# Attention plus SoLU block on one core: VectorE's block turns write contiguous runs, and the readers of the result take strides

## The chip, the cores and the metric

The kernel runs on one core of a Trainium2 chip. The metric is the device time of one execution in microseconds (us). A core has TensorE (PE in the profile, its weight loads PEld), VectorE (DVE), ScalarE (ACT), GpSimd (POOL) and the queue that issues all transfers here (SP).

## The reference

Rotary attention of 4 x 8 heads over 576 positions of 64 elements, and then a two-layer block over the 2304 tokens that result:

```python
def rotate(x):
    x1, x2 = (x[..., :half], x[..., half:])
    return np.concatenate([x1 * cos - x2 * sin, x1 * sin + x2 * cos], axis=-1)
scores = scale * np.matmul(rotate(q), rotate(k).transpose(0, 1, 3, 2))
attn = softmax(scores)                      # max subtracted, 1e-9 in the sum
x = (attn @ v)  -> 2304 tokens x 512
h = x @ w_in                                # 512 -> 1024
solu = h * softmax(h)
ln = (solu - mu) / np.sqrt(var + 1e-06) * g_ln
out = ln @ w_out                            # 1024 -> 512
```

All inputs and outputs are float32.

## The kernel before, in words

**Attention.** Heads are taken in 16 pairs (P = 0 to 15), one head in the upper and one in the lower 64 partitions. For each pair there are four tiles of 128 queries per head and one packed tile with the last 64 queries of both heads. A tile's scores go to PSUM (tiles pd, lines 408, 430, 433), VectorE takes the negated row maximum (mx, line 388), and ScalarE writes the exponentials to SBUF (tiles e, line 390, keys along the free axis). The second product needs them with keys on the partitions, so each 128 x 512 block of e is turned into ET (four key groups m of 128 keys each) and the last 64 keys into EL. `av` (lines 509 to 527) then multiplies v by ET and EL into a PSUM tile pg, and VectorE scales the result with the reciprocal row sums Rb into xT (line 525), which holds the tokens of a batch along the free axis. `av` runs twice per pair: r = 0 for 256 queries and r = 1 for 320 (two tiles and the packed one).

**Two ways to turn a tile.** For pairs 0 to 3, TensorE transposes four 128 x 128 blocks into pg (`tr`, line 448) and a copy brings them to ET (line 318 where ScalarE copies, line 320 where VectorE does). For pairs 4 to 15 the turn goes over DRAM (line 467 writes e to escr in 32-row groups, line 468 reads it back regrouped), and VectorE finishes it with one STREAM_TRANSPOSE of 32 x 32 blocks (line 469). In those the source is read in steps of four words (`p (j b m)`, m inner), and the destination is written in steps of four words as well (`p m (a j)`, j inner), so that the queries come out in their natural order. The last 64 keys (EL, `turn_last`) go over TensorE and a copy in all pairs.

**The block behind it.** For each of 18 tiles of 128 tokens, `front` splits x into two parts xh and xl, multiplies by w_in (line 590), and computes the SoLU into u. u goes to DRAM (uscr) and comes back regrouped into wraw; `back` turns it with two STREAM_TRANSPOSEs into tiles tb (line 642: read contiguously, written in steps of four words), copies the first part (lnh, lines 318 or 320) and subtracts it for the second (lnl, line 652, on GpSimd or VectorE), multiplies by w_out (line 660), and scales into the output (line 665).

**What sets the order.** A planner fixed one list for all engines (`ORDER`), which engine takes an operation that two may do (`FLIP`), and which buffer each tile gets (`BUFS`). These tables are written out in the kernel, each engine works its part in that order, and the costs in the calls of `add` (1040 and 1050 ns for the two transposes) only served the planner.

Of the kernel before, what the change touches and what calls it, by code (L numbers as in the profile page):

```python
# [12 lines left out]
ALU = mybir.AluOpType  # L13
# [158 lines left out]
class Plan:  # L172
# [22 lines left out]
    def buf(self, use):  # L195
        return self.pools[self.uses[use][0]][self.uses[use][2]]

    def add(self, eng, cost, prio, fn, r=(), w=(), use=(), xfer=0.0, alt=None, two=False, mode=0):
        i = len(self.ops)
        if alt is not None:  # L200
            self.alts[i] = (eng, cost) + alt
        deps = set()
        for k in r:
            if k in self.lastw:
                deps.add(self.lastw[k])
        for k in w:
            if k in self.lastw:
                deps.add(self.lastw[k])
            deps.update(self.readers.get(k, ()))
        deps.discard(i)  # L210
        for k in w:
            self.lastw[k] = i
            self.readers[k] = []
        for k in r:
            if k not in w:
                self.readers.setdefault(k, []).append(i)
        self.tags.append(self.tag)
        self.two.append(two)
        self.modes[i] = mode
        uses = (use,) if isinstance(use, int) else tuple(use)  # L220
        for u in uses:
            self.uses[u][1] += 1
        self.ops.append((eng, cost, prio, fn, deps, uses, xfer))
        return i


def dve(n):
    return 69 + n / 0.96
# [6 lines left out]
def act(n, ptrs=0, psum=True):  # L235
    return (51 if psum else 93) + n / 1.2 + 93 * ptrs
# [7 lines left out]
def kernel(  # L244
# [13 lines left out]
    nc = tc.nc  # L258
# [16 lines left out]
    def st(shape, dt, name):  # L275
        return sb.tile(shape, dt, name=name)
# [12 lines left out]
    ET = [st([128, 2, 4, n], F32, f"ET{i}") for i, (_, n) in enumerate(RNG)]  # L289
    EL = [st([128, n], F32, f"EL{i}") for i, (_, n) in enumerate(RNG)]  # L290
    xT = st([128, KC, RING], F32, "xT")
    Rb = st([128, S], F32, "Rb")
# [21 lines left out]
    add, use, buf = pl.add, pl.use, pl.buf  # L314

    def copy(e, o, i):
        if e is nc.scalar:
            nc.scalar.copy(o, i)  # L318
        else:
            e.tensor_copy(o, i)  # L320
# [7 lines left out]
    def tau(P, un):  # L328
        return TP[P] + PT[P] * un / 9
# [46 lines left out]
    def attention(P):  # L376
        par = P % 2
        b, c = divmod(P, PB)
        xoff = (b % 2) * S
# [59 lines left out]
        def chunk(e, m):  # L439
            return e.rearrange("p (x m) -> p m x", m=4)[:, m, :]  # L440
# [13 lines left out]
        def turn_tile(i, h):  # L454
            jt = 5 * P + i
            ej = et[jt % NE]
            r, q0 = divmod(i, 2)
            q0 *= 128
            base = 0 if h == 0 else S + 64
            pl.tag = f"T{P}.{i}.{h}"  # L460
            t = tau(P, 2 * i + h)
            if (i, h) in OFFS[P]:


                e, ke = ej[:, base:base + 512], ("e", jt % NE, h)
                sc, ks = escr[P, i, h], ("es", P, i, h)
                dma(t, sc.rearrange("i p c -> p i c"), e.rearrange("p (i c) -> p i c", i=4), 0, [ke], [ks], xf=728.0)
                dma(t, e, sc.rearrange("i (a j) c -> (i a) (j c)", j=4), 0, [ks], [ke], xf=728.0)
                add("dve", 1040, t, lambda: nc.vector.transpose(  # L469
                    ET[r][:, h, :, q0:q0 + 128].rearrange("p m (a j) -> p j m a", j=4),  # L470
                    e.rearrange("p (j b m) -> p j m b", j=4, m=4)), [ke], [("E", r, h, i % 2, 0)])
                return

            def blocks(bt):
                return [(bt[:, 128 * m:128 * m + 128], chunk(ej[:, base:base + 512], m)) for m in range(4)]

            tr(tau(P, 2 * i + h), [("e", jt % NE, h)], blocks, 512,
               [(ET[r][:, h, :, q0:q0 + 128], lambda bt: bt.rearrange("p (m q) -> p m q", m=4))], ("E", r, h, i % 2))

        def turn_last(r):  # L480

            pl.tag = f"T{P}.{r}.l"
            js = [(5 * P + 2 * r + y) % NE for y in range(2)]

            def blocks(bt):
                return [(bt[:, 128 * y:128 * y + 128], et[js[y]][:, S - 64:S + 64]) for y in range(2)]

            tr(tau(P, 4 * r + 3), [("el", j, h) for j in js for h in range(2)], blocks, 256,
               [(EL[r][:, 0:256], lambda bt: bt[:, 0:256])], ("EL", r, 0))

        def turn_packed():
            jt = 5 * P + 4
# [16 lines left out]
        def av(r, t):  # L509
            q0, nq = RNG[r]  # L510
            pl.tag = f"A{P}.{r}"
            ek = {h: [("E", r, h, y, 0) for y in range(2)] + ([("E", 1, "P", 0)] if r else []) for h in range(2)}
            lk = [("EL", r, 0, 0)] + ([("EL", 1, "P", 0), ("EL", 1, "P", 1)] if r else [])
            uy = use("G")
            yk = ("Y", uy)
            for m in range(5):
                def AV(m=m):
                    for h, rows in ((0, A), (1, B)):
                        e = ET[r][:, h, m, :] if m < 4 else EL[r]
                        nc.tensor.matmul(buf(uy)[rows, 0:nq], vv[:, m, h, :], e, start=(m == 0), stop=(m == 4))  # L520

                keys = ek[0] + ek[1] if m < 4 else lk
                add("pe", 2 * (nq * 2 / 2.4 + 3), t, AV, keys + [("v", par)], [yk], use=uy, mode=3)

            add("dve", dve(nq), t, lambda: nc.vector.tensor_tensor(  # L525
                xT[:, c, xoff + q0:xoff + q0 + nq], buf(uy)[:, 0:nq], Rb[:, q0:q0 + nq], op=ALU.mult),
                [yk] + [("R", r, j) for j in range((2, 3)[r])], [("x", b % 2, c, r)], use=uy)

        def norm(r, t):
# [33 lines left out]
    kl = [[("lh", z)] for z in range(2)], [[("ll", z)] for z in range(2)]  # L563
# [59 lines left out]
    def back(i, t, dur, tail):  # L623

        r0 = 128 * i
        tl = t + dur * 0.7
        col, mk = msc(i)
        pl.tag = f"l{i}"  # L630
        v = wraw.rearrange("p (j c) -> p j c", j=4)
        add("sp", 500, tl, lambda: nc.sync.dma_start(wraw, uscr[i].rearrange("i (a j) c -> (i a) (j c)", j=4)),
            [("us", i)], [("wr",)], xfer=2100.0)
        for z in range(2):
            pl.tag = f"t{i}.{z}"
            ub = use("B")
            bk = ("tz", ub)

            def turned(ub=ub):
                return buf(ub).rearrange("p (m t) -> p m t", m=4)  # L640

            add("dve", 1050, tl, lambda z=z, turned=turned: nc.vector.transpose(  # L642
                turned().rearrange("p m (a j) -> p j m a", j=4),
                v[:, :, 128 * z:128 * z + 128].rearrange("p j (m b) -> p j m b", b=32)),
                [("wr",), ("tbfree",)], [bk], use=ub)
            hd, ld = lh[:, 4 * z:4 * z + 4, :], ll[:, 4 * z:4 * z + 4, :]
            add("act", act(512, psum=False), tl, lambda e, hd=hd, turned=turned: copy(e, hd, turned()), [bk], kl[0][z], use=ub,
                alt=("dve", dve2(512)), two=True)
            c = [("pool", pool(512)), ("dve", dve(512))]
            if tail and z:  # L650
                c.reverse()
            add(*c[0], tl, lambda e, hd=hd, ld=ld, turned=turned: e.tensor_tensor(ld, turned(), hd, op=ALU.subtract),  # L652
                [bk] + kl[0][z], kl[1][z], use=ub, alt=c[1], two=True)
        pl.tag = f"o{i}"
        uo = use("G")
        ok = ("op", i)
        for f in range(FC):
            def mm2(f=f):
                for j, (a, w) in enumerate(((lh, woh), (lh, wol), (ll, woh))):
                    nc.tensor.matmul(buf(uo), a[:, f, :], w[:, f, :], start=(f == 0 and j == 0), stop=(f == FC - 1 and j == 2))  # L660
            add("pe", 3 * 228, t + dur + dur * 0.5 * f / FC, mm2, kl[0][f // 4] + kl[1][f // 4] + [("wo", f)], [ok], use=uo)
        to = t + 1.5 * dur
        add("act", act(512, 1, psum=False), to, lambda: nc.scalar.activation(osb, wm, AF.Copy, scale=col(13)), [("wm",)] + mk(13),
            [("o",)])
        add("dve", dve(512), to, lambda: nc.vector.scalar_tensor_tensor(  # L665
            osb, buf(uo), col(14), osb, op0=ALU.mult, op1=ALU.add), [ok, ("o",)] + mk(14), [("o",)], use=uo)
        dma(to, out[r0:r0 + 128, :], osb, 128 * DM * 4, [("o",)], [("out", i)])
# [129 lines left out]
    with tc.manual_schedule():  # L797
        for i in ORDER:
            if i in pl.alts:
                a = pl.alts[i]  # L800
# [67 lines left out]
```

## Time and profile before

| | us |
|---|---|
| median of 3 runs | 467.17 |
| lowest, highest | 464.99, 470.39 |
| span of the profiled execution, from its first to its last instruction | 464.3 |
| VectorE busy in it | 406.7 |
| TensorE busy in it | 436.2 |
| ScalarE, GpSimd busy in it | 264.1, 200.9 |

The profile is of one execution. Its span is 2.9 us below the median of the runs, which contains what lies around the span. Busy time is the union of an engine's instructions; matmuls are pipelined and their ends are modelled, so TensorE counts as busy also where it is not at its peak.

### The profile page before, as it was taken

How to read it: one execution, taken by the hardware profiler on the slowest of the kernel's cores; microseconds unless marked ns; L12 is line 12 of the kernel's file. 1: busy time of each engine (PE TensorE's matmuls, PEld its weight loads, DVE VectorE, ACT ScalarE, POOL GpSimd, SP SyncE). 2: the span in 40 equal slices, each digit the busy share in tenths (PEclk: the TensorE clock that was granted, in tenths of full speed). 3: DMA queues.
4: the chain of work that ended last, by engine and by line, in shares of the span. 5: the costliest groups of instructions: out<-in, count | busy, mean ns of one | idle time of the engine just before them, and what ended most of it. 6: DMA issues, size and time to landing. Idle time of an engine off the chain costs nothing.

```text
span 464.3 us, 7958 instructions
## 1 busy us (share of the span) xinstructions
PE 436.2 (94%) x2688; PEld 310.5 (67%) x2688; DVE 406.7 (88%) x663; ACT 264.1 (57%) x597; POOL 200.9 (43%) x164
## 2 busy tenths in 40 slices
PE   1799999999999979999999999999999999999996
PEld 1456666677667755766667677666767676778885
DVE  3889999999989999899999999999999889796672
ACT  1568898888766557455646545464655544433421
POOL 1203342435778355437458465656365320102331
PEclk9989999999999999999999999999999999999999
DMA  7547465799879999999889899999799787643541
GB/s 240 184 145 241 146 221 179 235 265 315 261 229 298 287 282 276 291 324 301 282 239 305 260 292 309 294 321 286 241 272 327 242 244 234 201 139 114 158 160 46
DMA packets 96410, 112.42 MB, mean 242 GB/s; under 512 B 7649, under 2 KB 71153, under 8 KB 96369
## 3 DMA queue, kind: packets, MB, share of 16 engines
q1 hardware_dynamic: 96368, 111.91, 76.9%
q8 instruction: 21, 0.34, 0.3%
q14 instruction: 21, 0.16, 0.1%
HBM read 72.49 MB, written 39.40 MB: 241 GB/s over the span
## 4 chain that ended last, share of the span: by engine, by line
PE 25%; DMA 13%; DVE 11%; ACT 2%; issue 2%; SPq 1%; DVEq 0%; ACTq 0%
PE pg L660 9%; PE pd L590 9%; DMA escr<-e 5%; DMA e<-escr 4%; PE pg L520 3%; DVE ET L469 3%; PE pd L408 2%; DVE mx L388 2%; DMA wraw<-uscr 2%; DVE ms L597 1%; PE pg L448 1%; DMA Rb<-rscr 1%; DMA uscr<-u 1%; DVE tb L642 1%; ACT e L390 1%
## 5 line engine op out<-in xcount | busy, mean ns | idle before, releaser
L390 ACT ACTIVATE e<-pd,mx 128x576 f32<-128x576 f32 x144 | 106.2, 739 | 73.6 <-DVE mx L388 52.1
L469 DVE STREAM_TRANSPOSE ET<-e 128x512 f32<-128x512 f32 x96 | 105.6, 1132 | 8.9 <-DMA e<-escr 8.4
L388 DVE TENSOR_REDUCE mx<-pd 128x1 f32<-128x576 f32 x144 | 103.5, 743 | 8.1 <-PE pd L408 7.0
L520 PE MATMUL pg<-ET,vst 128*64 128x256 f32 (+1 forms) x512 | 71.5, 418 | 0.9 <-DVE o L665 0.4
L652 POOL TENSOR_TENSOR lnl<-tb,lnh 128x512 fp32r<-128x512 f32 x30 | 38.7, 1290 | 61.4 <-ACT lnh L318 33.7
L590 PE MATMUL pd<-wih,xh 128*128 128x512 f32 x144 | 60.1, 417 | 0.5 <-ACT e L390 0.5
L660 PE MATMUL pg<-woh,lnh 128*128 128x512 f32 x144 | 58.8, 408 | 1.1 <-DVE xT L525 0.4
L590 PE MATMUL pd<-wih,xl 128*128 128x512 f32 x144 | 56.5, 392 | 0.0
L660 PE MATMUL pg<-woh,lnl 128*128 128x512 f32 x144 | 56.3, 391 | 0.0
L590 PE MATMUL pd<-wil,xh 128*128 128x512 f32 x144 | 56.2, 391 | 0.0
L660 PE MATMUL pg<-wol,lnh 128*128 128x512 f32 x144 | 56.2, 390 | 0.0
L448 PE MATMUL pg<-idn,e 128*128 128x128 f32 (+1 forms) x272 | 50.3, 300 | 5.6 <-ACT e L390 2.7
L520 PEld LDWEIGHTS pg<-ET,vst 128*64 128x64 f32 x512 | 34.7, 138 | 26.4 <-issue 4.6
L448 PEld LDWEIGHTS pg<-idn,e 128*128 128x128 f32 (+1 forms) x272 | 36.7, 187 | 23.4 <-ACT e L390 5.6
L642 DVE STREAM_TRANSPOSE tb<-wraw 128x512 f32<-128x512 f32 x36 | 39.0, 1099 | 1.8 <-DMA wraw<-uscr 1.6
L408 PE MATMUL pd<-kh,qh 64*128 64x288 f32 x192 | 38.0, 344 | 1.7 <-ACT e L390 0.7
L408 PE MATMUL pd<-rotk,rotq 64*128 64x288 f32 x128 | 27.0, 502 | 10.7 <-DVE rotk L349 9.7
L349 POOL TENSOR_TENSOR rawk<-rawk,tabs 128x576 f32<-128x576 f32 (+1 forms) x21 | 29.2, 1397 | 12.5 <-DMA rawk<-in_k_t_dram 12.5
L660 PEld LDWEIGHTS pg<-woh,lnh 128*128 128x128 f32 x144 | 27.1, 188 | 9.5 <-issue 2.1
L590 PEld LDWEIGHTS pd<-wih,xh 128*128 128x128 f32 x144 | 27.1, 188 | 9.3 <-issue 2.1
L349 POOL TENSOR_TENSOR rawq<-rawq,tabs 128x576 f32<-128x576 f32 x20 | 28.8, 1448 | 10.5 <-DMA rawq<-in_q_t_dram 10.5
L599 ACT ACTIVATE u<-pd,ms 128x1024 f32<-128x1024 f32 x18 | 20.1, 1116 | 22.1 <-DVE ms L597 10.6
(101 smaller groups left out, 841.8 us busy)
## 6 DMA issues: line engine op xcount, KB each, us to landing
escr<-e SPq DMA_DIRECT2D x96, 256.0 KB
e<-escr SPq DMA_DIRECT2D x96, 256.0 KB
uscr<-u SPq DMA_DIRECT2D x18, 512.0 KB
wraw<-uscr SPq DMA_DIRECT2D x18, 512.0 KB
rawq<-in_q_t_dram SPq DMA_DIRECT2D x15, 576.0 KB
rawk<-in_k_t_dram SPq DMA_DIRECT2D x15, 576.0 KB
vst<-in_v_t_dram SPq DMA_DIRECT2D x16, 320.0 KB
out_dram<-o SPq DMA_DIRECT2D x18, 256.0 KB
```

Of the source, the lines that this page charges most:

```text
L349: add(*c[0], prio, lambda e: e.tensor_tensor(o, a, b, op=op), r, w, alt=c[1], two=True)
L388: add("dve", 672, t, lambda: nc.vector.tensor_reduce(mx[:, mcol:mcol + 1], buf(us)[:, :, 0:288], axis=AX.XY, op=ALU.max, negate=True), [sk ...
L390: add("act", 720, t, lambda: nc.scalar.activation(e.rearrange("p (z n) -> p z n", z=2), buf(us)[:, :, 0:288], AF.Exp, bias=mx[:, mcol:mcol ...
L408: nc.tensor.matmul(buf(us)[:, z, 0:288], a[rows, c0:c0 + 128], w[rows, 288 * z:288 * z + 288], start=(j == 0), stop=(j == len(terms) - 1))
L448: nc.tensor.transpose(dst, src, idn)
L469: add("dve", 1040, t, lambda: nc.vector.transpose(ET[r][:, h, :, q0:q0 + 128].rearrange("p m (a j) -> p j m a", j=4), e.rearrange("p (j b ...
L520: nc.tensor.matmul(buf(uy)[rows, 0:nq], vv[:, m, h, :], e, start=(m == 0), stop=(m == 4))
L590: nc.tensor.matmul(buf(uh)[:, z, :], a[:, c, :], w[:, c, HF * z:HF * z + HF], start=(c == 0 and j == 0), stop=(c == KC - 1 and j == 2))
L599: add("act", act(DFF, 2), tm, lambda: nc.scalar.activation(u, buf(uh), AF.Exp, bias=col(2), scale=1.0, accum_out=col(3)), hf + mk(2), ku + ...
L642: add("dve", 1050, tl, lambda z=z, turned=turned: nc.vector.transpose(turned().rearrange("p m (a j) -> p j m a", j=4), v[:, :, 128 * z:128 ...
L652: add(*c[0], tl, lambda e, hd=hd, ld=ld, turned=turned: e.tensor_tensor(ld, turned(), hd, op=ALU.subtract), [bk] + kl[0][z], kl[1][z], use ...
L660: nc.tensor.matmul(buf(uo), a[:, f, :], w[:, f, :], start=(f == 0 and j == 0), stop=(f == FC - 1 and j == 2))
```

## The change

The destination of each STREAM_TRANSPOSE is laid out as (j, a) in place of (a, j): each block of 32 columns is written as one contiguous run. In ET the columns of a 128-query group are then no longer in query order. So that both ways of turning agree, the copies from TensorE's transposes into ET and EL read PSUM in steps of four words and write contiguously, and the scaling into xT puts the order right: it reads pg in steps of 32 words, and, for r = 1, takes the 64 packed queries (which keep their order) in a second instruction. The tiles tb keep the new order as well, so lnh and lnl read tb in steps of 32 words. `ORDER`, `FLIP`, `BUFS` and the costs stay as they are.

```diff
                 add("dve", 1040, t, lambda: nc.vector.transpose(
-                    ET[r][:, h, :, q0:q0 + 128].rearrange("p m (a j) -> p j m a", j=4),
+                    ET[r][:, h, :, q0:q0 + 128].rearrange("p m (j a) -> p j m a", j=4),
                     e.rearrange("p (j b m) -> p j m b", j=4, m=4)), [ke], [("E", r, h, i % 2, 0)])
...
-               [(ET[r][:, h, :, q0:q0 + 128], lambda bt: bt.rearrange("p (m q) -> p m q", m=4))], ("E", r, h, i % 2))
+               [(ET[r][:, h, :, q0:q0 + 128].rearrange("p m (j a) -> p m j a", j=4),
+                  lambda bt: bt.rearrange("p (m a j) -> p m j a", m=4, j=4))], ("E", r, h, i % 2))
...
-               [(EL[r][:, 0:256], lambda bt: bt[:, 0:256])], ("EL", r, 0))
+               [(EL[r][:, 0:256].rearrange("p (y j a) -> p y j a", y=2, j=4),
+                  lambda bt: bt[:, 0:256].rearrange("p (y a j) -> p y j a", y=2, j=4))], ("EL", r, 0))
...
-            add("dve", dve(nq), t, lambda: nc.vector.tensor_tensor(
-                xT[:, c, xoff + q0:xoff + q0 + nq], buf(uy)[:, 0:nq], Rb[:, q0:q0 + nq], op=ALU.mult),
+            def scale():
+                o, y_, f = xT[:, c, xoff + q0:xoff + q0 + nq], buf(uy)[:, 0:nq], Rb[:, q0:q0 + nq]
+                nc.vector.tensor_tensor(
+                    o[:, 0:256].rearrange("p (t a j) -> p t a j", t=2, j=4),
+                    y_[:, 0:256].rearrange("p (t j a) -> p t a j", t=2, j=4),
+                    f[:, 0:256].rearrange("p (t a j) -> p t a j", t=2, j=4), op=ALU.mult)
+                if r:
+                    nc.vector.tensor_tensor(o[:, 256:nq], y_[:, 256:nq], f[:, 256:nq], op=ALU.mult)
+
+            add("dve", dve(nq), t, scale,
...
-                return buf(ub).rearrange("p (m t) -> p m t", m=4)
+                return buf(ub).rearrange("p (m j a) -> p m a j", m=4, j=4)
...
-                turned().rearrange("p m (a j) -> p j m a", j=4),
+                buf(ub).rearrange("p (m j a) -> p j m a", m=4, j=4),
...
-            add("act", act(512, psum=False), tl, lambda e, hd=hd, turned=turned: copy(e, hd, turned()), [bk], kl[0][z], use=ub,
+            add("act", act(512, psum=False), tl, lambda e, hd=hd, turned=turned: copy(e, hd.rearrange("p m (a j) -> p m a j", j=4), turned()), [bk], kl[0][z], use=ub,
...
-            add(*c[0], tl, lambda e, hd=hd, ld=ld, turned=turned: e.tensor_tensor(ld, turned(), hd, op=ALU.subtract),
+            add(*c[0], tl, lambda e, hd=hd, ld=ld, turned=turned: e.tensor_tensor(
+                ld.rearrange("p m (a j) -> p m a j", j=4), turned(), hd.rearrange("p m (a j) -> p m a j", j=4), op=ALU.subtract),
```

The only instructions that are added are the second scalings: VectorE gets 16, one per pair. On VectorE at the end of a pair in the early part, before the change (L525 is the scaling, the first for r = 1 and the second for r = 0 of the next pair):

```order
L534 TENSOR_SCALAR acc_101<-acc_101 128x5
L388 TENSOR_REDUCE mx<-pd_116 128x1
L349 TENSOR_TENSOR rawq<-rawq,tabs 128x576
L388 TENSOR_REDUCE mx<-pd_115 128x1
L535 RECIPROCAL acc_101<-acc_101 128x5
L525 TENSOR_TENSOR xT<-pg_119,Rb 128x320
L525 TENSOR_TENSOR xT<-pg_118,Rb 128x256
L388 TENSOR_REDUCE mx<-pd_117 128x1
```

The same place on VectorE after the change, where L529 and L534 are the two parts of the scaling and the reciprocal has moved to line 545:

```order
L544 TENSOR_SCALAR acc_101<-acc_101 128x5
L388 TENSOR_REDUCE mx<-pd_116 128x1
L349 TENSOR_TENSOR rawq<-rawq,tabs 128x576
L388 TENSOR_REDUCE mx<-pd_115 128x1
L545 RECIPROCAL acc_101<-acc_101 128x5
L529 TENSOR_TENSOR xT<-pg_119,Rb 128x256
L534 TENSOR_TENSOR xT<-pg_119,Rb 128x64
L529 TENSOR_TENSOR xT<-pg_118,Rb 128x256
L388 TENSOR_REDUCE mx<-pd_117 128x1
```

The 320-wide scaling is now one of 256 and one of 64 columns behind each other; everything else stands in the same place, on this engine and on the others.

## Rows read from the trace of the kernel before

**Rows 1.** The page: busy tenths of two engines in 40 slices of the span.

```profile
PE   1799999999999979999999999999999999999996
...
DVE  3889999999989999899999999999999889796672
```

**Rows 2.** Windows: stretch and length, busy us of PE, PEld, DVE, ACT, POOL, PEclk, DMA, GB/s.

```profile
16.00:100.00 84.00, 80.56 (x530) 53.81 (x529) 79.43 (x149) 66.08 (x159) 26.27 (x19) 0.98 0.63 201
100.00:400.00 300.00, 290.07 (x1868) 206.01 (x1866) 276.25 (x425) 172.47 (x394) 157.27 (x123) 0.99 0.89 278
400.00:465.00 65.00, 60.28 (x280) 47.70 (x278) 43.42 (x76) 21.52 (x38) 14.82 (x15) 1.00 0.40 128
```

**Rows 3.** Waits of the whole span: us in total, times, longest.

```profile
ACT e L390 <- DVE mx L388: 52.1, 39, 5.4
...
POOL lnl L652 <- ACT lnh L318: 33.7, 16, 6.2
...
DVE mx L388 <- PE pd L408: 7.0, 15, 1.1
```

**Rows 4.** Lines 469 and 642: shortest, median and longest of their transposes in ns.

```profile
L469 DVE STREAM_TRANSPOSE ET<-e x96: 1068/1134/1186, 101.8 to 408.6; 128x512 f32<-128x512 f32 x96
...
L642 DVE STREAM_TRANSPOSE tb<-wraw x36: 1049/1098/1194, 125.6 to 452.5; 128x512 f32<-128x512 f32 x36
```

**Rows 5.** Groups by form, VectorE, whole span: busy us, mean ns, idle before.

```profile
L525 DVE TENSOR_TENSOR xT<-pg,Rb 128x320 f32<-128x320 f32 x16 | 7.7, 481 | 1.6 <-DMA Rb<-rscr 0.8 <-PE pg L520 0.7
...
L525 DVE TENSOR_TENSOR xT<-pg,Rb 128x256 f32<-128x256 f32 x16 | 6.6, 413 | 2.4 <-DMA Rb<-rscr 2.1 <-ACT ET L318 0.2
...
L349 DVE TENSOR_TENSOR xl<-xT,xh 128x512 fp32r<-128x512 f32 x5 | 3.5, 690 | 0.1
...
L741 DVE SCALAR_TENSOR_TENSOR xT<-tb,xT 128x512 uint32<-128x512 uint32 x4 | 2.7, 684 | 0.0
```

**Rows 6.** Groups by form, GpSimd and ScalarE, whole span.

```profile
L652 POOL TENSOR_TENSOR lnl<-tb,lnh 128x512 fp32r<-128x512 f32 x30 | 38.7, 1290 | 61.4 <-ACT lnh L318 33.7 <-DVE lnh L320 20.2 <-PE pd L408 7.5
...
L318 ACT CAST lnh<-tb 128x512 fp32r<-128x512 f32 x25 | 15.4, 615 | 11.1 <-DVE tb L642 7.9 <-DVE ms L616 2.3 <-PE pg L660 0.5
```

**Rows 7.** Groups by form, 16 to 100 us, the copies and scalings.

```profile
L318 ACT COPY ET<-pg 128x512 f32<-128x512 f32 x33 | 18.9, 589 | 7.1 <-PE pg L448 7.1
...
L318 ACT COPY EL<-pg 128x256 f32<-128x256 f32 x8 | 3.0, 372 | 1.4 <-PE pg L448 1.4
...
L320 DVE COPY ET<-pg 128x512 f32<-128x512 f32 x3 | 2.1, 686 | 0.1
...
L525 DVE TENSOR_TENSOR xT<-pg,Rb 128x256 f32<-128x256 f32 x4 | 1.7, 419 | 0.2 <-ACT ET L318 0.2
...
L525 DVE TENSOR_TENSOR xT<-pg,Rb 128x320 f32<-128x320 f32 x3 | 1.4, 467 | 0.7 <-PE pg L520 0.7
```

**Rows 8.** Groups by form, 100 to 400 us, VectorE.

```profile
L469 DVE STREAM_TRANSPOSE ET<-e 128x512 f32<-128x512 f32 x93 | 102.3, 1132 | 8.8 <-DMA e<-escr 8.4
...
L642 DVE STREAM_TRANSPOSE tb<-wraw 128x512 f32<-128x512 f32 x25 | 27.1, 1102 | 0.9 <-DMA wraw<-uscr 0.9
...
L525 DVE TENSOR_TENSOR xT<-pg,Rb 128x320 f32<-128x320 f32 x12 | 5.8, 483 | 0.8 <-DMA Rb<-rscr 0.8
...
L525 DVE TENSOR_TENSOR xT<-pg,Rb 128x256 f32<-128x256 f32 x12 | 4.9, 411 | 2.3 <-DMA Rb<-rscr 2.1
...
L320 DVE COPY EL<-pg 128x256 f32<-128x256 f32 x7 | 2.9, 417 | 0.7 <-PE pg L448 0.7
...
L320 DVE CAST lnh<-tb 128x512 fp32r<-128x512 f32 x4 | 1.6, 412 | 0.0
```

**Rows 9.** The chain that ended last: start us, us, what.

```profile
438.62 21.77 PE pg L660 x96
```

**Rows 10.** Timeline of VectorE's last instructions: start us, us, instruction.

```profile
454.80 0.43 DVE L320 CAST lnh<-tb 128x512 fp32r<-128x512 f32 x1 [1.17 <-PE pg L660]
...
455.81 0.68 DVE L652 TENSOR_TENSOR lnl<-tb,lnh 128x512 fp32r<-128x512 f32 x1
```

More of the change, by code (lines that the diff above doesn't have):

```diff
@@ L639, in turned @@
             def turned(ub=ub):
-                return buf(ub).rearrange("p (m t) -> p m t", m=4)
-            add("dve", 1050, tl, lambda z=z, turned=turned: nc.vector.transpose(
-                turned().rearrange("p m (a j) -> p j m a", j=4),
+                return buf(ub).rearrange("p (m j a) -> p m a j", m=4, j=4)
+            add("dve", 1050, tl, lambda z=z, ub=ub: nc.vector.transpose(
+                buf(ub).rearrange("p (m j a) -> p j m a", m=4, j=4),
                 v[:, :, 128 * z:128 * z + 128].rearrange("p j (m b) -> p j m b", b=32)),
```

## The prediction

> **What bounds the kernel now.** I read the slices of the page first [rows 1]. TensorE and VectorE are both near nine tenths from about 30 us on, and VectorE falls off only in the last fifth. Three stretches with different work come out of this, and the windows give their sums [rows 2]. From 16 to 100 us (pairs 0 to 3, turned on TensorE; the weights are prepared beside them) VectorE is busy for 79.4 of 84 us, ScalarE for 66.1. From 100 to 400 us (pairs 4 to 15 with their turns over DRAM) VectorE is busy for 276.3 of 300 us, and TensorE, with its modelled ends, for 290.1. After 400 us TensorE alone runs on. The waits say the same [rows 3]: the longest sum is ScalarE's, 52.1 us for VectorE's row maxima, while VectorE waits for scores for only 7.0 us. So VectorE's time counts in the first two stretches, with TensorE close behind it in the second; at the end it does not.
>
> **The transposes.** STREAM_TRANSPOSE takes 93 x 1132 ns and 25 x 1102 ns in the middle stretch, 47% of VectorE's busy time there [rows 8]. The two differ in one thing: line 642 reads contiguously and writes in steps of four words, line 469 does both in steps of four words. A contiguous two-input operation on as many elements takes 690 ns [rows 5]. So there are 1102 - 690 = 412 ns, 0.80 ns per element, that may be the price of the steps or may belong to the transpose itself. No row shows a transpose without a strided side. For line 642 after the change the bounds are 1102 ns (no gain) and 690 ns; a copy that reads and writes SBUF contiguously takes 412 ns [rows 8], and I keep that as the far end. I take 690, because the shortest of the 36 (1049 ns) is 145 ns below the longest [rows 4], a spread that suits a wait for memory. For line 469 the write becomes contiguous and the read keeps its steps. Its bounds are 1132 and 690. A second strided side costs 30 ns more than one, so the two sides hide behind each other, and with one left I take 1102.
>
> [...]
>
> **The strided readers.** They read one word in four (the copies to ET and EL) or one in 32 (xT, lnh, lnl). The bounds for an element are 0 (line 741 reads every second word and takes 684 ns, no more than the 690 of the contiguous one [rows 5]) and the transposes' 0.80 ns; below nothing is excluded, since no reader has fewer elements than before. I take 0.80, because the step of the copies is the same four words, and keep 0 for the range.
>
> **Middle stretch, VectorE** [rows 8]. Saved: 25 x 412 ns = 10.3 us and 93 x 30 ns = 2.8 us, together 13.1. Added: 24 scalings x 256 x 0.80 ns = 4.9; the second scaling of r = 1, of which the columns were there before, so that only the fixed part is new: from 481 ns at 320 and 413 at 256 [rows 5] a column costs 1.06 ns and the fixed part is 413 - 272 = 141 ns, 12 times 1.7 us; seven copies to EL x 0.205 = 1.4; four casts to lnh, which take two elements at a time, x 0.205 = 0.8. Together 8.8, so VectorE gains 4.3 us; with free readers 11.4. How much becomes time: TensorE is busy in 290.1 of the 300 us [rows 2], and once VectorE is earlier its matmuls are late next. I take half, between none and all: -2.1 us (free readers -5.7). ScalarE gets more to do (25 casts to lnh in the whole run, 0.41 us each [rows 6]), but it has 127 us idle in this stretch [rows 2]. GpSimd's 30 subtractions [rows 6] may grow by 0.41 us each; it sits idle for 61.4 us before them, waiting mostly for lnh [rows 3]. I cost both at nothing; if that cover were gone, 25 casts x 0.41 = 10 us and 30 subtractions x 0.41 = 12 us would be at stake.
>
> **Early stretch** [rows 7]. There are no transposes on VectorE here, so there is nothing to gain. VectorE gets 7 x 0.205 = 1.4, 3 x 0.141 = 0.4 and at most 3 x 0.41 = 1.2, together 3.0 us, on an engine that is 95% busy. ScalarE gets 0.41 us for each copy of a tile (29 of its 33; the other four are packed and unchanged), 11.9 us, and 8 x 0.205 = 1.6 for EL: 66.1 + 13.5 = 79.6 of 84 us. It waits for TensorE's transposes before these copies now (7.1 us), so most is covered, but TensorE needs ET and the pg buffers back. I take VectorE's 3.0 and one more: +4.0 us. With free readers it is the second scalings alone, +0.4.
>
> **End.** The chain ends with 96 matmuls of 21.77 us, 227 ns each, without a gap [rows 9]. They end at 460.4 us, so the last 12 start at 457.7. The last subtraction ends at 455.81 + 0.68 = 456.5 us [rows 10], 1.2 us early. With 0.2 us more in the cast and 0.41 in the subtraction it is still early, even without a faster transpose: nothing.
>
> **Sum.** -2.1 + 4.0 = +1.9 us on the profiled span: 464.3 + 1.9 = 466.2. The median of the runs is 2.9 us above that span, so the forecast is 469 us. Between the chosen ends, with 0.40 ns per element in place of 0.80, it would be about 1.8 us below the median of before. A measurement of this kernel tells about 1% (4.7 us) from no change; the forecast lies inside. Its own range is 462 to 476: lower if all of VectorE's gain becomes time and TensorE follows, higher if ScalarE's 13.5 us come through in the early stretch.
>
> **Rivals.**
>
> First, the readers are free and the transposes gain as above: -5.7 + 0.4 = -5.3, 462 us. For it speaks line 741; against it, that its step is two words and not four or 32.
>
> Second, line 469 falls to 690 ns too, because only writes pay: 93 x 442 ns = 41.1 and 10.3 saved, 8.8 added, so VectorE would be busy for 234 of 300 us. Then TensorE and the transfers bound that stretch. TensorE's row leaves 10 us of idle, half of VectorE's gain would be 21; I take 16, and with +4 early it is 455 us. For it speaks that 1132 and 1102 are almost one number although one reads with steps and the other does not; against it, that a hidden price shows once the cover is gone.
>
> Third, slower: the transposes' time is their own and none of them gets faster, and the readers pay. VectorE then has 8.8 us more in the middle stretch, where it rarely waits for anything, and all of it becomes time; with +4.0 early it is +12.8, 480 us. It decides from the point where the transposes save less than 8.1 us together (8.8 - 8.1 + 4.0 = 4.7). For it speaks that the two lines differ by only 3% with different source patterns, as a fixed rate would; against it, the shortest ones.
>
> Fourth, the layout costs nothing anywhere, in transposes or readers, and the change does not do what it says: only the 15 second scalings of the two stretches stay, 2.1 us, 469 us.
>
> **How the numbers follow.** I give the forecast 0.35, the first rival 0.14, the second 0.22, the third 0.22, the fourth 0.07. Faster by over 1%: 0.05 + 0.09 + 0.20 = 0.34. Slower by over 1%: 0.10 from the forecast's upper part, 0.18 from the third, 0.01 from the fourth = 0.29. Within 1%: the remaining 0.37. The range of 450 to 482 holds the forecast and the third rival's value and reaches 5 us below the second's; what is left out is a VectorE gain that passes to the end in full, and a ScalarE that binds the early stretch on top of the third rival.
>
> **What would show it right or wrong.** Line 652 (the former 642) near 690 ns and line 469 near 1100 ns; the scaling of 256 columns near 620 ns and ScalarE's copy to ET near 1000 ns; the window of the first 100 us some 4 us longer and the rest some 2 us shorter. The forecast is wrong if line 469 falls with the other, if line 652 stays where it was, or if the readers keep their times.

## The result: 471.0 us, less than 1% slower, and the profile after

| | before | after |
|---|---|---|
| median of 15 runs each, us | 467.70 | 471.00 |
| lowest, highest | 464.99, 470.39 | 468.90, 474.00 |
| span of the profiled execution | 464.3 | 470.1 |

The ratio is 1.0075, with a 95% interval of 1.0050 to 1.0099: about 3.5 us slower, small but outside the uncertainty. Ratios here and below leave out runs that took over 1.5% more than the fastest run of the same kernel. The spans of the two profiled executions are 5.8 us apart. Part of that is chance: 1.8 us of a run lie outside the span (the profiled run after took 471.87 us for its span of 470.1), so the run profiled after lies 0.9 us above its median and the one before 1.6 us below. The 2.9 us that the prediction put around the span were therefore 1.8 us and a profiled run that was faster than the median.

The busy times in the page of after, for all engines:

```profile
PE 436.4 (93%) x2688; PEld 310.5 (66%) x2688; DVE 402.4 (86%) x679; ACT 276.2 (59%) x597; POOL 209.6 (45%) x164
```

VectorE has 4.3 us less to do, ScalarE 12.1 and GpSimd 8.7 us more. TensorE's sum is the same to 0.2 us.

The operations that the change touches, in the view of lines by shape of after (operation, tiles, shapes, count, busy us, mean ns, idle before it); lines 469 and 652 answer to [rows 4] and [rows 8], the scalings to [rows 5], ScalarE's and GpSimd's rows to [rows 6] and [rows 7]:

```profile
L469 DVE STREAM_TRANSPOSE ET<-e 128x512 f32<-128x512 f32 x96 | 103.6, 1098 | 16.0 <-DMA e<-escr 15.7
L662 POOL TENSOR_TENSOR lnl<-tb,lnh 128x512 fp32r<-128x512 f32 x30 | 47.1, 1570 | 61.8 <-ACT lnh L318 44.4 <-DVE lnh L320 11.6 <-PE pd L408 5.7
L318 ACT CAST lnh<-tb 128x512 fp32r<-128x512 f32 x25 | 28.4, 1136 | 7.1 <-DVE tb L652 5.3 <-DVE ms L626 1.1 <-PE pg L671 0.5
L652 DVE STREAM_TRANSPOSE tb<-wraw 128x512 f32<-128x512 f32 x36 | 24.9, 698 | 2.4 <-POOL lnl L662 1.5 <-DMA wraw<-uscr 1.0
L318 ACT COPY ET<-pg 128x512 f32<-128x512 f32 x43 | 24.6, 586 | 8.3 <-PE pg L448 8.0
L529 DVE TENSOR_TENSOR xT<-pg,Rb 128x256 f32<-128x256 f32 x32 | 13.1, 410 | 3.8 <-DMA Rb<-rscr 2.0 <-PE pg L522 1.4
L318 ACT COPY EL<-pg 128x256 f32<-128x256 f32 x25 | 9.2, 370 | 9.7 <-PE pg L448 9.7
L320 DVE CAST lnh<-tb 128x512 fp32r<-128x512 f32 x11 | 8.3, 757 | 3.8 <-PE pg L671 3.7
L662 DVE TENSOR_TENSOR lnl<-tb,lnh 128x512 fp32r<-128x512 f32 x6 | 6.5, 1085 | 0.3
L534 DVE TENSOR_TENSOR xT<-pg,Rb 128x64 f32<-128x64 f32 x16 | 3.5, 216 | 0.5 <-DMA Rb<-rscr 0.5
```

The transposes came out as forecast, 698 and 1098 ns. The readers split in two groups. Those that read PSUM in steps (ET and EL on ScalarE, xT on VectorE, 586, 370 and 410 ns) take what they took; of the 43 copies to ET, 29 read in steps, and the longest of all takes 625 ns against 621 before. Those that read SBUF in steps are slower: the copy to lnh went from 615 to 1136 ns on ScalarE, the subtraction to lnl from 1290 to 1570 on GpSimd. VectorE's own share of the two went from 419 to 757 (11 copies) and from 699 to 1085 ns (6 subtractions). For half a tile these three stand behind each other: the transpose gives 0.40 us back, the copy on ScalarE takes 0.52 more and the subtraction 0.28 more.

The windows of after, columns as in [rows 2], for the two stretches that can be compared:

```profile
16.00:100.00 84.00, 78.12 (x517) 51.95 (x516) 78.73 (x149) 65.23 (x158) 26.47 (x19) 0.98 0.61 195
100.00:400.00 300.00, 288.09 (x1864) 204.80 (x1863) 270.44 (x438) 182.18 (x395) 163.57 (x123) 1.00 0.90 279
```

In the middle VectorE's work fell by 5.8 us, and TensorE's did not rise with it: it fell by 2.0 (1864 matmuls against 1868), so TensorE waited longer. Part of what it waited for is a row that before does not have at all. Its weight loads' waits for the two parts of ln, in the waits of after (waiting engine and line, what it waits for, us in total, times, longest):

```profile
PEld pg L671 <- POOL lnl L662: 1.4, 3, 0.9
PEld pg L671 <- DVE lnl L662: 0.7, 2, 0.5
PEld pg L448 <- ACT lnh L318: 0.5, 1, 0.5
...
PEld pd L408 <- ACT lnh L318: 0.4, 1, 0.4
PEld pg L671 <- ACT lnh L318: 0.2, 1, 0.2
```

Together 3.2 us, and the change costs about 3.5 us. The two need not be the same: between the two profiles TensorE's idle time grew by 5.6 us (from 464.3 - 436.2 to 470.1 - 436.4), so these waits are part of it. The last of them is in the end of the chain of after (start us, us, what), which answers to [rows 9] and [rows 10]:

```profile
446.88 0.60 DVE lnh L320
447.53 0.04 issue
447.57 1.12 DVE lnl L662
...
455.34 1.15 ACT lnh L318
456.49 0.07 issue
456.56 1.56 POOL lnl L662
458.12 0.04 issue
458.17 8.01 PE pg L671 x34
...
466.27 0.75 DVE o L676
```

The same copy and the same subtraction in the timelines of before, on ScalarE and on GpSimd:

```profile
449.38 0.62 ACT L318 CAST lnh<-tb 128x512 fp32r<-128x512 f32 x1
...
450.08 1.29 POOL L652 TENSOR_TENSOR lnl<-tb,lnh 128x512 fp32r<-128x512 f32 x1 [3.74 <-ACT lnh L318]
```

Before, TensorE ran its last 96 matmuls without a gap: the last 34 of them started at about 452.7 us (460.4 less 34 x 0.227), and this subtraction ended at 451.4, 1.3 us early. Now the last 34 start when GpSimd hands over lnl.

### The profile page after: what moved, and what is told of

It is laid out like the page before. It is cut to its first block, busy times and chain, and to the rows that moved or that the text cites. A ratio compares the mean times of both kernels' runs of the same rounds, so it can differ in the third digit from the quotient of the medians.

```text
span 470.1 us, 7966 instructions
## 1 busy us (share of the span) xinstructions
PE 436.4 (93%) x2688; PEld 310.5 (66%) x2688; DVE 402.4 (86%) x679; ACT 276.2 (59%) x597; POOL 209.6 (45%) x164
## 2 busy tenths in 40 slices
DMA packets 96409, 112.42 MB, mean 239 GB/s; under 512 B 7648, under 2 KB 71152, under 8 KB 96368
## 5 line engine op out<-in xcount | busy, mean ns | idle before, releaser
L469 DVE STREAM_TRANSPOSE ET<-e 128x512 f32<-128x512 f32 x96 | 103.6, 1098 | 16.0 <-DMA e<-escr 15.7
L662 POOL TENSOR_TENSOR lnl<-tb,lnh 128x512 fp32r<-128x512 f32 x30 | 47.1, 1570 | 61.8 <-ACT lnh L318 44.4
L408 PE MATMUL pd<-kh,qh 64*128 64x288 f32 x192 | 39.2, 344 | 1.7 <-ACT e L390 1.0
L408 PE MATMUL pd<-rotk,rotq 64*128 64x288 f32 x128 | 25.6, 476 | 11.3 <-DVE rotk L349 10.3
L408 PE MATMUL pd<-kl,qh 64*128 64x288 f32 x192 | 33.0, 298 | 0.0
L408 PEld LDWEIGHTS pd<-kh,qh 64*128 64x128 f32 x192 | 22.4, 184 | 16.2 <-issue 7.1
```

The costliest lines, as they stand in the source:

```text
L408: nc.tensor.matmul(buf(us)[:, z, 0:288], a[rows, c0:c0 + 128], w[rows, 288 * z:288 * z + 288], start=(j == 0), stop=(j == len(terms) - 1))
L469: add("dve", 1040, t, lambda: nc.vector.transpose(ET[r][:, h, :, q0:q0 + 128].rearrange("p m (j a) -> p j m a", j=4), e.rearrange("p (j b ...
```

## The experiments

The theory after this reading: the second block's half of the change costs, because the readers of tb became slower on ScalarE and GpSimd, and TensorE waits for lnh and lnl. The rivals: the attention half costs (the second scaling); or VectorE's time does count, and what it gained was lost elsewhere. Every run is compared with runs of the kernel before in the same session (medians there 466.89 to 467.57 us, 17 to 30 runs). The ratios are those on record; they differ somewhat from the quotients of the medians that stand beside them.

**One half of the change each.** The first takes over all that the change does to ET, EL and xT and leaves tb alone; the second does the reverse:

```diff
 first:
-                    ET[r][:, h, :, q0:q0 + 128].rearrange("p m (a j) -> p j m a", j=4),
+                    ET[r][:, h, :, q0:q0 + 128].rearrange("p m (j a) -> p j m a", j=4),
 second:
-                turned().rearrange("p m (a j) -> p j m a", j=4),
+                buf(ub).rearrange("p (m j a) -> p j m a", m=4, j=4),
```

> Only the attention half of the change (ET and EL in the new order, scaling in two parts); the turns of the second block, tb and its readers are as before. Theory A, the loss comes from the strided readers of tb: no loss left, VectorE gets 96 x 0.034 us less and 16 x 0.147 us more, net -0.9 us, so 466 to 469 us where before has 467.7. Theory B, the loss comes from the attention half (second scaling in the early stretch, where both profiles already differ by 2 us): 470 to 471.5 us.

Measured: 469.12 us, ratio 1.0046 (1.0012 to 1.0079). TensorE's loads waited 0.5 us for lnl.

> Only the half of the second block (tb written contiguously, lnh and lnl read it in steps of 32 words); attention as before. Theory A: the whole loss, 470 to 472 us. Theory B: no loss, 465 to 468 us, since VectorE's 36 transposes gain 0.4 us each.

Measured: 470.02 us, ratio 1.0065 (1.0032 to 1.0098). The end of its chain:

```profile
451.94 1.15 ACT lnh L318
453.08 0.07 issue
453.15 1.56 POOL lnl L652
454.71 0.04 issue
454.75 8.01 PE pg L661 x34
```

The second half alone brings the late subtraction and its 34 matmuls at the end, and loads that waited 3.3 us for lnh and lnl, as in after. It is the larger part. The first half seems to cost something too. The two ratios add up to 1.1%, more than the 0.75% of both together; the intervals allow that.

**Price and gain of the second block apart.** The first kernel keeps the strided write of the transpose and reads tb with strides all the same; the second writes contiguously and reads contiguously. In both the tokens of a tile leave in another order than the reference's; the work is otherwise the same.

```diff
 price without gain:
-                return buf(ub).rearrange("p (m t) -> p m t", m=4)
+                return buf(ub).rearrange("p (m j a) -> p m a j", m=4, j=4)
...
+                buf(ub).rearrange("p (m a j) -> p j m a", m=4, j=4),
 gain without price:
-                turned().rearrange("p m (a j) -> p j m a", j=4),
+                turned().rearrange("p m (j a) -> p j m a", j=4),
```

> As before, but lnh and lnl read tb in steps of 32 words while the transposes still write it in steps of four (the tokens of a tile leave in another order). The price of the readers without the gain of the transposes. Theory A: clearly worse than the whole change, 473 to 478 us, with the copies near 1.14 us and the subtractions near 1.57 us. Theory B: 467 to 469 us.

Measured: 471.68 us, ratio 1.0126 (1.0068 to 1.0185). The waits of TensorE's loads on ln in it:

```profile
PEld pg L661 <- POOL lnl L652: 2.8, 5, 0.9
PEld pg L661 <- DVE lnl L652: 1.1, 2, 0.8
PEld pg L448 <- ACT lnh L318: 0.5, 1, 0.5
PEld pd L408 <- ACT lnh L318: 0.4, 1, 0.4
PEld pg L661 <- ACT lnh L318: 0.2, 1, 0.2
```

> As before, but tb is written contiguously and lnh and lnl still read it contiguously (the tokens of a tile leave in another order). The gain of the 36 transposes (0.40 us each, 14.4 us of VectorE) without the price. Theory A: it becomes time in part, 462 to 466 us. Theory C, the fixed order lets no gain through because TensorE or the transfers are late next: 467 to 468.5 us, VectorE idle for some 14 us more.

Measured: 466.68 us, ratio 0.9970 (0.9928 to 1.0013). Its transposes to tb, and no wait on ln at all in its list:

```profile
L642 DVE STREAM_TRANSPOSE tb<-wraw 128x512 f32<-128x512 f32 x36 | 24.8, 698 | 1.3 <-POOL lnl L652 0.6 <-DMA wraw<-uscr 0.5
```

With before and the second half these make a square:

| us | readers contiguous | readers strided | readers' price |
|---|---|---|---|
| transposes to tb write in steps (1099 ns) | 467.4 | 471.7 | 4.3 |
| transposes to tb write contiguously (698 ns) | 466.7 | 470.0 | 3.3 |

14.2 us less transposing on VectorE (39.0 against 24.8) is worth 0.7 to 1.7 us by the medians, not told from nothing: the interval of gain without price holds 1, and those of the two kernels with strided readers overlap. The readers' price is 3 to 4 us in either row, and by the ratio of price without gain (six runs) 5.9 us. So the price is shown, and a gain is not: by the lower end of its interval (0.9928) at most some 3.4 of the 14 us became time.

**The attention half: the second scaling.** The first kernel is before with the scaling in two pieces and nothing else. The second is the attention half with the columns of ET and EL ordered by j over all columns of an `av`, the packed queries included, so that one scaling of 256 or 320 columns does again.

```diff
 only the split:
+                nc.vector.tensor_tensor(o[:, 0:256], y_[:, 0:256], f[:, 0:256], op=ALU.mult)
+                if r:
+                    nc.vector.tensor_tensor(o[:, 256:nq], y_[:, 256:nq], f[:, 256:nq], op=ALU.mult)
 no split:
-                    ET[r][:, h, :, q0:q0 + 128].rearrange("p m (a j) -> p j m a", j=4),
+                    ET[r][:, h].rearrange("p m (j a) -> p j m a", j=4)[:, :, :, q0 // 4:q0 // 4 + 32],
```

> As before in every layout, only the scaling of r = 1 is issued as two instructions of 256 and 64 columns. Theory A, the attention half loses by its second scaling (16 x 0.147 us on VectorE, and the pg buffer is released later for TensorE): 468.5 to 470 us where before has 467.4. Theory B, it loses by something else in the new order of ET: 467 to 468 us.

Measured: 469.04 us, ratio 1.0021 (0.9983 to 1.0060).

> The attention half of the change with the columns of ET and EL ordered by j over all of an av (runs of 32 or 16 queries), so that one scaling of 320 columns suffices; second block as before. Theory A: the loss of e1 is gone and the 96 x 0.034 us of the transposes stay, 465.5 to 467.5 us. Theory B: like e1, 468.5 to 470 us.

Measured: 466.25 us, ratio 0.9975 (0.9941 to 1.0009). Without the split the attention half costs nothing that can be measured; with it, it cost 0.46%. The split by itself cannot be told from nothing. So the second scaling may be the cause of the 2 us of that half, but no run shows it. The mean granted TensorE clock of the runs was 0.9975 without the split and 0.9945 in the attention half; by the relation of time and clock found below, 1.1 us of the difference between these two go with the clock.

**Another payer: the transfers.** If the order is to be put right neither by the transposes nor by their readers, the transfer of u to DRAM can do it: four transfers per tile with permuted rows in place of one. The transposes to tb and their readers are then both contiguous and the tokens leave in their order.

```diff
-        add("sp", 500, td, lambda: nc.sync.dma_start(uscr[i].rearrange("i p c -> p i c"), uf.rearrange("p (i c) -> p i c", i=4)),
+        def spill():
+            for x in range(4):
+                nc.sync.dma_start(uscr[i][x].rearrange("(a j) c -> j a c", j=4), uf[:, 256 * x:256 * x + 256])
+
+        add("sp", 500, td, spill,
```

> tb written contiguously and read contiguously, in the right order of tokens: u goes to DRAM in four transfers per tile, whose rows are put so that the read back brings every 32nd token's neighbour into one run; 54 more transfers, the same bytes; attention as before. If the new transfers cost nothing: like e4, 463 to 467 us. If the queue or smaller transfers hold up the second block: 468 us or more, with longer waits for wraw.

Measured: 523.96 us, ratio 1.1213 (1.1157 to 1.1270). The waits of the queue that issues the transfers, and of ScalarE for the buffer of u, in this kernel:

```profile
SPq L636 <- DMA uscr<-u: 58.3, 28, 5.6
...
ACT u L599 <- DMA uscr<-u: 35.9, 8, 7.8
```

That wait of the queue before:

```profile
SPq L632 <- DMA uscr<-u: 14.9, 9, 3.0
```

The queue waits 58.3 us for the transfers of u in place of 14.9, with everything else that it issues behind them, and ScalarE waits 35.9 us to overwrite u. The trace says more: packets and bytes are the same in both pages (96410 and 112.42 MB), but during the last tile's transfers of u the 16 DMA engines are busy for 0.29 of the time in place of 0.98 (last two columns: DMA share and GB/s; the first line is this kernel, the second before):

```profile
503.70:506.70 3.00, 3.00 (x15) 2.48 (x14) 2.06 (x6) 0.72 (x1) 1.80 (x2) 1.00 0.29 90
...
443.40:444.90 1.50, 1.50 (x8) 1.23 (x8) 1.40 (x6) 0.93 (x3) 0.36 (x1) 1.00 0.98 339
```

The read back of that tile is issued 8.0 us after its first write, against 5.1 us before. So the engines stood idle for 0.71 of the time of these transfers, in place of 0.02; how many of them a transfer uses is not shown. Whether the size of a new transfer or its pattern, which begins with a dimension of four rows, is the reason was not separated.

The second kernel joins this with the attention half without a split:

> e6 and e7 together: contiguous writes of all 132 transposes, no strided reader of SBUF, one scaling. VectorE gets 96 x 0.034 + 36 x 0.40 = 17.7 us less and nothing more. Theory A: 462 to 466 us, below before. Theory C, the fixed order lets no gain through: 467 to 468 us.

Measured: 525.74 us, ratio 1.1244 (1.1184 to 1.1303): the transfers decide here too. One of its six runs took 1045.39 us, for a reason that nothing on record shows; the ratio leaves it out.

**Where the second block's half is paid.** It was done for the last five tiles alone (the ones behind the last pair), and for the other 13 alone:

```diff
 last five:
+                return buf(ub).rearrange("p (m j a) -> p m a j" if tail else "p (m a j) -> p m a j", m=4, j=4)
...
 first 13:
+                return buf(ub).rearrange("p (m j a) -> p m a j" if not tail else "p (m a j) -> p m a j", m=4, j=4)
```

> The half of the second block only for the 5 token tiles of the last batch (10 of 36 transposes, their 10 copies and 10 subtractions), everything else as before. Theory A1, the price of tb's readers is paid at the end, where the chain transpose, copy, subtraction stands ahead of TensorE with about 1 us to spare: 468.5 to 470 us where before has 467.5, with TensorE waiting for lnl after 440 us. Theory A2, it is paid in the middle: 467 to 468 us.

Measured: 469.58 us, ratio 1.0038 (1.0000 to 1.0075); loads waiting for lnl 1.8 us.

> The half of the second block for the 13 token tiles of the first three batches only. Theory A1: no loss, 465.5 to 467.5 us, since VectorE gains 26 x 0.40 us there and ScalarE and GpSimd have idle time. Theory A2: 468.5 to 470 us.

Measured: 470.16 us, ratio 1.0064 (1.0024 to 1.0103); loads waiting for lnh and lnl 1.4 us. Both parts cost, the first by an interval that just reaches 1. In the waits they make up the whole (1.8 + 1.4 = 3.2 us, against 3.3 with both); in the times they add up to more than it, within the intervals. So it is paid both at the end and in the middle, and the shares stay open.

**Does VectorE's time count at all?** To the attention half without a split this kernel adds a contiguous read for line 469: in pairs 4 to 15 the key groups are 32 neighbouring keys, and v is laid out to suit. The packed tile's exponential becomes two instructions, of which the first reads PSUM in steps of 32 words, and VectorE gets twelve small additions (2.8 us) for their row sums.

```diff
-                    e.rearrange("p (j b m) -> p j m b", j=4, m=4)), [ke], [("E", r, h, i % 2, 0)])
+                    e.rearrange("p (j m b) -> p j m b", j=4, m=4)), [ke], [("E", r, h, i % 2, 0)])
```

> e6 with the reads of line 469 made contiguous as well: in pairs 4 to 15 a key group is 32 neighbouring keys (v is laid out for it, the packed tile is put in that order by ScalarE's exponential, which reads PSUM in steps of 32 words, in two instructions). If strides are what makes a transpose slow: ET's transposes at 690 to 710 ns, VectorE 96 x 0.41 = 39 us less busy, and a time of 445 to 460 us, more than half of it given back to TensorE and the transfers. If a transpose that is read in steps has its time from something else: 1100 ns and 466 us as e6.

Measured: 468.59 us, ratio 1.0017 (0.9980 to 1.0054). The row of its 96 transposes and its window of the middle:

```profile
L489 DVE STREAM_TRANSPOSE ET<-e 128x512 f32<-128x512 f32 x96 | 64.7, 692 | 19.3 <-DMA e<-escr 19.3
...
100.00:400.00 300.00, 290.32 (x1880) 206.91 (x1880) 247.62 (x439) 175.01 (x417) 157.15 (x123) 1.00 0.89 278
```

The transposes take 40.9 us less than before (64.7 against 105.6), VectorE is busy for 28.6 us less in the middle stretch, and the time does not move beyond its uncertainty. The idle time only changes its name: VectorE now waits 19.3 us for the transfers before line 469 (8.4 before) and 12.5 us for scores (7.0 before, [rows 3]). TensorE's 290.3 us of the 300 stay. So VectorE's time is not the bound, unless the instructions that this kernel adds hide a gain. TensorE's work in its fixed order, 436 us in all, is the likeliest bound; this is read and not shown, since no kernel here shortens TensorE. The transfers, at 0.89 of the 16 DMA engines in this window as before, are a rival that no run takes work off, and so is the order itself, which no run changed. The clock speaks for TensorE: over 195 runs of before and ten of these kernels (the change and those with the split transfers left out), 1% more granted TensorE clock goes with 3.6 +- 0.7 us less time, nearly the 4.4 us that 1% of 436 is. It is no proof, because the clock may also follow the waits: in the split transfers' kernel, where TensorE is busy for 87% of the span in place of 94%, the granted clock is 0.96.

**Copies or subtractions.** The last kernel is the price without gain again, but only the copy to lnh reads tb with strides; lnl subtracts contiguously. (The expectation says that the tokens leave in another order and that lnl is then no remainder. That was a mistake: lnh and lnl still add up to tb element by element, and the output is the reference's to rounding.)

```diff
-                ld.rearrange("p m (a j) -> p m a j", j=4), turned(), hd.rearrange("p m (a j) -> p m a j", j=4), op=ALU.subtract),
+                ld, buf(ub).rearrange("p (m t) -> p m t", m=4), hd, op=ALU.subtract),
```

> e3 with the subtractions reading contiguously again: only the 36 copies to lnh read tb in steps of 32 words, the transposes write in steps of four as before (the tokens leave in another order, and lnl is not the remainder of lnh). Theory D, the price of the readers comes in by ScalarE, whose 25 copies stand 0.52 us longer in front of exponentials and of the subtractions: 470 to 472 us, as e3. Theory E, it comes in by GpSimd's and VectorE's subtractions, the last step before TensorE: 467 to 468.5 us, as before.

Measured: 469.29 us, ratio 1.0028 (0.9993 to 1.0062). It lies between the theories and settles nothing: the copies may carry part of the price and the subtractions the rest.

**All runs in one table.** TensorE's loads' waits for lnh and lnl, from each profile, beside the cost that the ratio gives (1% is 4.7 us):

| kernel | loads wait for ln, us | ratio | cost, us |
|---|---|---|---|
| gain without price | 0 | 0.9970 | -1.4 |
| attention half, no split | 0 | 0.9975 | -1.2 |
| scaling split only | 0 | 1.0021 | 1.0 |
| no split, contiguous keys | 0.4 | 1.0017 | 0.8 |
| attention half | 0.5 | 1.0046 | 2.1 |
| second block, first 13 tiles | 1.4 | 1.0064 | 3.0 |
| second block, last 5 tiles | 1.8 | 1.0038 | 1.8 |
| copies only | 2.2 | 1.0028 | 1.3 |
| the change | 3.2 | 1.0075 | 3.5 |
| second block | 3.3 | 1.0065 | 3.0 |
| price without gain | 5.0 | 1.0126 | 5.9 |

Each cost is uncertain by 1.2 to 2.8 us and each wait is of one run (that of copies only is the longest of its twelve, 473.04 us), so single rows say little. But the three longest waits stand beside the three largest costs (the first 13 tiles' is level with the third), and where no load waits the cost is not told from nothing. No kernel tried here is faster than before by more than its uncertainty.

## Why the prediction was right, and where its steps were not

The forecast of 469.0 us and its own range of 462 to 476 hold the 471.0. That the number fits is luck: the sum of +1.9 us was near the 3.5 through terms that were wrong on both sides. One of the prediction's own signs of being wrong came true, since the readers of PSUM kept their times. Its split of the time failed too: it had the first 100 us some 4 us longer and the rest 2 us shorter. The transposes of line 469 after (shortest, median and longest in ns, first and last start):

```profile
L469 DVE STREAM_TRANSPOSE ET<-e x96: 1034/1101/1192, 103.8 to 413.1; 128x512 f32<-128x512 f32 x96
```

The first starts at 103.8 us in place of 101.8 [rows 4], and the rest of the span is 3.8 us longer. The 2.0 us of the early stretch cannot be told from chance: in six kernels that run the same instructions as before up to there, that transpose starts between 99.8 and 104.7 us.

- **The transposes** were right: line 652 at 698 ns (690 forecast), line 469 at 1098 (1102), and the reading behind it too, that two strided sides hide behind each other: line 469 took 1132 ns with both sides strided, 1098 with one, and 692 with both contiguous. The price is (1098 - 692) / 512 = 0.79 ns per element for the one side that was left.
- **The readers' price of 0.80 ns for all readers** failed. It is zero for the three that read PSUM: 586 ns against 587 for the copy to ET, where 1000 was forecast, 410 against 413 for the scaling, where 620 was, and 370 against 371 for ScalarE's copy to EL. It is (1136 - 615) / 512 = 1.02 for ScalarE from SBUF, (1570 - 1290) / 512 = 0.55 for GpSimd. For VectorE's own subtraction it is (1085 - 699) / 512 = 0.75, and its copies to lnh grew by 338 ns in the mean, from 419 to 757, where 205 were forecast; no run shows that they take two elements at a time, from which the 205 was worked out. The six subtractions were left out of the sum. The step that failed is that one price was taken for two memories and three engines. The first rival, free readers, was right for PSUM and wrong for SBUF.
- **Early stretch, +4.0 us**: all but the three second scalings (410 + 216 - 481 = 145 ns each, 141 forecast) rested on PSUM readers and falls away. So ScalarE's 13.5 us, the reason for the upper end of the range, never came.
- **Middle, half of VectorE's gain becomes time**: failed. VectorE gained 5.8 us there (4.3 forecast), and neither these nor the 14.2 and 40.9 us of two experiments can be told in the time. The prediction read the longest wait, ScalarE's 52 us for row maxima, as the mark of the bound. Those waits are those of an engine with much idle time; TensorE, at 290 of 300 us, which the text names as close behind, was the one to ask about first.
- **ScalarE's and GpSimd's growth costed at nothing**: failed, and this is where most of the loss is. The growth was 25 x 0.52 = 13.0 and 30 x 0.28 = 8.4 us, near the 10 and 12 us that the text had at stake "if that cover were gone". Their idle time is an average; the three steps of a half tile form a chain, and where TensorE needs lnl soon after, the chain's own length counts. Of these 21 us and VectorE's 6 on the same steps (11 x 0.34 and 6 x 0.39), 3 to 4 come through, by the waits (3.2 us) and the square.
- **End, nothing**: failed. The cast and the subtraction that [rows 10] show had 1.2 us of slack, and after they are still early: VectorE's last subtraction starts at 461.86 us and takes 1.09, and the last 12 matmuls start at about 463.5. The prediction looked at this last pair alone. The subtraction that TensorE now waits for is an earlier one, on GpSimd behind a copy on ScalarE. It had 1.3 us of slack; these two grew by 0.80 us, and the chain ahead of them, which goes back through copies and subtractions that grew as well, took the rest.
- **The third rival**, at 480 us, was wrong in its reason, since the transposes did get faster, and right in its sign.

## What to carry to other kernels

Someone has to read or write with steps when the order of elements changes: try it first where PSUM is read, which cost nothing here (586 against 587 ns on ScalarE, 410 against 413 on VectorE), and not where another engine reads SBUF (1136 against 615 ns on ScalarE, 1570 against 1290 on GpSimd). An engine at nine tenths need not be the bound (VectorE was busy for 276 of 300 us in the middle, and 28.6 us less of it did not show in the time): take work off it, as two experiments did, before counting its saving as time. And an engine with 40% idle time, as ScalarE has here (264 of 464 us busy), is no cover for a chain of three short steps that TensorE waits for; look at who waits for the last of them.

## What had not been expected of the hardware

- ScalarE and VectorE read PSUM here in steps of 4 and 32 words at the time of contiguous reads: 586 against 587 ns for 512 elements on ScalarE, 410 against 413 for 256 on VectorE.
- Two engines at the same time. The profile of the attention half loses 1.2 us at 57 us for a reason that has nothing to do with strides. VectorE's timeline, before:

```profile
56.98 0.68 DVE L349 TENSOR_TENSOR wil<-xT,wih 128x512 fp32r<-128x512 f32 x1
```

GpSimd's timeline, before:

```profile
57.04 1.89 POOL L349 TENSOR_TENSOR rawq<-rawq,tabs 128x576 f32<-128x576 f32 x1 [5.55 <-DMA rawq<-in_q_t_dram]
```

VectorE's timeline, attention half:

```profile
57.08 1.90 DVE L349 TENSOR_TENSOR wil<-xT,wih 128x512 fp32r<-128x512 f32 x1
```

GpSimd's timeline, attention half:

```profile
57.02 1.41 POOL L349 TENSOR_TENSOR rawq<-rawq,tabs 128x576 f32<-128x576 f32 x1 [5.43 <-DMA rawq<-in_q_t_dram]
```

Both operations have two inputs in SBUF. Before, VectorE starts 0.06 us ahead and GpSimd's takes 1.89 us in place of some 1.4; in the other kernel GpSimd is 0.06 us ahead and VectorE's takes 1.90 in place of 0.68. After has the 1.90 too. In all 14 profiles VectorE's takes 0.68 or 0.69 us where it starts first or level (six) and 1.90 to 1.92 where GpSimd is first (eight). So of these two the one that starts later pays, some 0.5 us on GpSimd or 1.2 on VectorE; by what mechanism is not shown. Since 0.1 us decides, single profiles differ by this much without a cause in the change: of seven kernels that run the same instructions up to there, before among them, VectorE is first in three and GpSimd in four.
- Each transfer of u, 512 KB, in four of 128 KB with permuted rows, on a queue that everything else uses, cost 12% of the whole time, with the same packets and bytes: during the last tile's, the 16 DMA engines were busy for 0.29 of the time, in place of 0.98.
